# A three-stage attention and feed-forward kernel: another order of loads, operand splitting and cluster similarities ahead of the first attention step

## The chip, the cores and the metric

One core of one Trainium2 chip. The metric is the device time of one execution in microseconds (us); the time before is the median of 3 runs. In the traces PE is the matrix engine, PEld its weight loads, DVE the vector engine, ACT the scalar engine, POOL the GpSimd engine and SP the engine that only issues transfers. A q behind a name (SPq, POOLq) is that engine's instruction queue.

## What is computed

Three stages in one launch, in float32. The cut below shows the first, which the change is in; the other two are a low-rank token mixing with a ReLU feed-forward, and a feed-forward gated by a convolution.

```python
# q, k, v: (2, 8, 768, 64); centroids: (8, 16, 64)
q_assign = np.argmax(np.einsum('bhsd,hcd->bhsc', q_n, c_n), axis=-1)   # rows normalised
k_assign = np.argmax(np.einsum('bhsd,hcd->bhsc', k_n, c_n), axis=-1)
mask = q_assign[:, :, :, None] == k_assign[:, :, None, :]
scores = np.where(mask, scale * (q @ k.transpose(0, 1, 3, 2)), -1e9)
attn = softmax(scores)
x = (attn @ v), heads side by side           # (2, 768, 512)
u = x + (x.T @ U @ V).T;  y = u + relu(u @ w_ch1) @ w_ch2
h = relu(y @ w_in);       out = (h * sigmoid(conv3(h))) @ w_out
```

## The kernel before, in words

There are 2 batches of 8 heads; two neighbouring heads form a **pair**, so there are 8 pairs (p 0 to 3 of batch 0, then of batch 1). A head has 768 queries in 6 tiles of 128, so attention has 96 **steps**, 12 for a pair; step n is written out by `step(n)` (L545). The schedule is written by hand: each engine runs its instructions in the order of the program text and stops at the first one whose inputs are not there.

Products of float32 numbers are made from a rounded part (the type fp32r, written high) and the exact rest (low). For a head the scores' operands lie in two tiles. `ab` (128 rows) holds, for q and k, one high part and one low rest; `cd` (80 rows) holds the high parts and 16 more rows, the one-hot of the cluster that a token belongs to. A score tile is two matmuls on `ab` (L250) and two on `cd` (L252), summed in one bank pair `sc`; one for each half of the 768 keys.

A pair's operands come about so:

- `load_raw` (L87): three SP transfers bring the pair's q rows (`rq`, 384 KB) and k rows (`rk`, two of 192 KB on 64 partitions each).
- `load_ops` (L96): three POOL transfers, of 384 KB at the source each, bring one head's rows as fp32r into `ab` (twice) and `cd`. `split_ops` (L114) subtracts to get the low rests in `ab`.
- `sims` (L182): 24 small matmuls of `rq` and `rk` with the centroids (`cbq`, `cbk`) give the similarities. `sims_onehot` (L193) turns them into one-hots in five DVE operations, `onehot_t` (L212) transposes these on PE, and `onehot_rows` (L219) puts them into `cd`. For the first head of all (`first=True`) ACT writes both rows directly; otherwise ACT makes `os` and SP transfers move it.
- `load_v` (L105): one SP transfer (`rv`) and two POOL transfers (`vt`) for the values.

Ahead of the steps stands a prologue. SP loads the centroids and pair 0's rows; POOL makes `identf`, then issues the six `load_ops` transfers of heads 0 and 1 and two of `vt`. `warm(count)` (L134) issues that many matmuls whose result nothing reads, on zeroed data; there are 13 and 4 of them around the transpose of the centroids (L160) and 16 behind the similarities. DVE normalises the centroids, copies them into `cbq` and `cbk` (L163 to L166), writes constants (L169 to L177), makes head 0's low rests (L433 calls `split_ops` with DVE) and the one-hots. POOL makes head 1's low rests and those of `vt` (L436).

In step n the order on PE is: scores of n+2 (`s_mm`), value product of an earlier group (`pv_mm`), at s = 2 of a pair the similarities of the next pair (L563), and the transposes of n (`t_mm`, L280). DVE runs the low rests of n-1 (L293) and the score maximum of n+2 (`s_max`, L259); ACT the copies of n-1 (L289) and the exponential of n+1 (L271). `prep(n)` (L512) then issues what the next pair needs: s = 0 loads rows and the first head's operands, s = 2 to 5 one-hot parts, splits, `load_v` and the second head's operands, s = 7 the one-hot rows. `pump` moves the float64 weights of the later stages through SP, ACT, DVE and POOL, one piece at a time.

Of the kernel before, what the change touches and what calls it, by code (L numbers as in the profile page):

```python
# [15 lines left out]
F32 = mybir.dt.float32  # L16
# [8 lines left out]
P = 128  # L25
# Score offset that removes a key of another cluster. It exceeds every score by so
# much that a query whose cluster holds no key sees equal scores everywhere.
# [4 lines left out]
def tile_kernel(ctx: ExitStack, tc: tile.TileContext, qk, vv, cen, u_w, v_w, w1, w2, win, wout, conv, out):  # L32
# [20 lines left out]
    # ---- right side: u^T of the first batch, x rows, first weights, staging  # L53
# [9 lines left out]
    # ---- attention pools; the operands of the scores on top, to be freed first  # L63
# [18 lines left out]
    # ---------------------------------------------------------------- loads  # L82
# [12 lines left out]

    def load_ops(b, p, j):  # L96
        h = 2 * p + j
        ab = a_ab.tile([P, 2, S], F32R, tag="ab", name="ab")
        cd = a_ab.tile([80, 2, S], F32R, tag="cd", name="cd")
        nc.gpsimd.dma_start(out=ab[0:D], in_=qk[b, h])  # L100
        nc.gpsimd.dma_start(out=ab[D:2 * D], in_=qk[b, h])
        nc.gpsimd.dma_start(out=cd[0:D], in_=qk[b, h])
        ops[b, h] = (ab, cd)
# [17 lines left out]
    # ------------------------------------------------------------- constants  # L121
    cent = acon.tile([P, 2, D], F32, name="cent")
    nc.sync.dma_start(out=cent[:, 0], in_=cen)
    load_raw(0, 0)
    identf = const.tile([P, P], F32, name="identf")
    make_identity(nc, identf)
    load_ops(0, 0, 0)

    # TensorE runs at half its clock until it has been busy for a few microseconds
# [14 lines left out]
    # centroids, normalised, transposed into block-diagonal stationaries  # L144
# [7 lines left out]
    nc.scalar.activation(early, cn[:, 1:2], AF.Exp)  # brings Exp's table in before the scores  # L152
# [15 lines left out]
    identb = const.tile([P, P], BF16, name="identb")  # L168
    nc.vector.tensor_copy(identb, identf)  # L169
    iota = acon.tile([P, NT * 4, NC], BF16, name="iota")  # L170
    for c in range(NC):
        nc.vector.memset(iota[:, :, c:c + 1], float(NC - c))
    ohs = acon.tile([2 * 2 * NC, 2], F32, name="ohs")
    nc.vector.memset(ohs[0:2 * NC, 0:1], 1.0)
    nc.vector.memset(ohs[0:2 * NC, 1:2], 0.0)
    nc.vector.memset(ohs[2 * NC:4 * NC, 0:1], BIG)
    nc.vector.memset(ohs[2 * NC:4 * NC, 1:2], -BIG)  # L177

    # ------------------------------------------- cluster assignment of a pair
# [13 lines left out]
    def sims_onehot(b, p, part):  # L193
        """One-hot of the first largest similarity, in five parts."""
        sh = [P, NT * 4, NC]
        v = ohst[b, p]
        if part == 0:
            v["mx"] = a_oh.tile([P, NT * 4, 1], F32, tag="mx", name="mx")
            nc.vector.tensor_reduce(out=v["mx"], in_=v["pm"], axis=AX.X, op=ALU.max)
        elif part == 1:  # L200
            v["eq"] = a_oh.tile(sh, BF16, tag="eq", name="eq")
            nc.vector.tensor_tensor(out=v["eq"], in0=v["pm"], in1=v["mx"].to_broadcast(sh), op=ALU.is_ge)
        elif part == 2:
            nc.vector.tensor_tensor(out=v["eq"], in0=v["eq"], in1=iota, op=ALU.mult)
        elif part == 3:
            v["m2"] = a_oh.tile([P, NT * 4, 1], BF16, tag="m2", name="m2")
            nc.vector.tensor_reduce(out=v["m2"], in_=v["eq"], axis=AX.X, op=ALU.max)
        else:
            v["oh"] = a_oh.tile(sh, BF16, tag="oh", name="oh")
            nc.vector.tensor_tensor(out=v["oh"], in0=v["eq"], in1=v["m2"].to_broadcast(sh), op=ALU.is_equal)  # L210
# [8 lines left out]
    def onehot_rows(b, p, first=False):  # L219
        pt = ohst.pop((b, p))["pt"]  # L220
        if first:
            cd = ops[b, 2 * p][1]
            nc.scalar.activation(cd[D:D + NC, 0], pt[0:NC], AF.Copy)
            nc.scalar.activation(cd[D:D + NC, 1], pt[2 * NC:3 * NC], AF.Copy, scale=BIG, bias=-BIG)  # L224
        os_ = a_oh.tile([4 * NC, S], F32R, tag="os", name="os")
        nc.scalar.activation(os_, pt, AF.Identity, scale=ohs[:, 0:1], bias=ohs[:, 1:2])
        for j in range(1 if first else 0, 2):
            cd = ops[b, 2 * p + j][1]
            for i in range(2):
                r0 = (2 * i + j) * NC  # L230
                nc.sync.dma_start(out=cd[D:D + NC, i].bitcast(F32), in_=os_[r0:r0 + NC].bitcast(F32))

    # ----------------------------------------------------- attention, by steps
# [10 lines left out]
    def s_mm(n):  # L244
        b, h, t = head_of(n)
        ab, cd = ops[b, h]
        ps = ps_s.tile([P, 2, 512], F32, tag="s", name="sc")
        c0 = t * P
        for f in range(2):
            nc.tensor.matmul(ps[:, f, 0:HS], ab[:, 0, c0:c0 + P], ab[:, 1, f * HS:(f + 1) * HS], start=True, stop=False)  # L250
        for f in range(2):
            nc.tensor.matmul(ps[:, f, 0:HS], cd[0:80, 0, c0:c0 + P], cd[0:80, 1, f * HS:(f + 1) * HS], start=False, stop=True)  # L252
        st["s", n] = ps
# [85 lines left out]
    # ------------------------------------------------------------- weights  # L339
    # The parameters come as float64 words (low, high). The high word read as a  # L340
    # float32 and scaled by 2^-112 has the exponent rebased; shifted left by three
    # and joined with the sign and the low word's top bits it is the float32.
# [39 lines left out]
    # stages by ticks after a block's start: thinly spread, or one block every two ticks  # L382
# [3 lines left out]
    def pump(plan):  # L386
        """Moves every parameter block in flight on by a tick and starts the next one."""
# [37 lines left out]
    # ------------------------------------------------- the attention schedule  # L425
    sims(0, 0)
    load_ops(0, 0, 1)
    split_ops(0, 0, 0, nc.vector)
    warm(16)
    for part in range(5):  # L430
        sims_onehot(0, 0, part)
    onehot_t(0, 0)
    onehot_rows(0, 0, first=True)  # L433
    rv0 = load_v(0, 0)
# [3 lines left out]
    # parameters of the later stages  # L438
# [20 lines left out]
    # ---- token mixing, u = x + V^T (U^T x), and u^T split: in units that share a bank  # L459
# [52 lines left out]
    def prep(n):  # L512
        """Work for the next pair of heads, spread over this pair's twelve steps."""
        pair, s = divmod(n, 2 * NT)
        nxt = pair + 1
        if nxt < B * NP:
            b, p = divmod(nxt, NP)
            for part, at in enumerate((2, 2, 3, 4, 5)):
                if s == at:
                    sims_onehot(b, p, part)  # L520
            if s == 0:
                load_raw(b, p)
# [22 lines left out]
    def step(n):  # L545
# [17 lines left out]
        if s == 2 and n < NQ and pair + 1 < B * NP:  # L563
# [32 lines left out]
    # ---- u + relu(u W1) W2, in quarters of the hidden features  # L596
# [43 lines left out]
    def ffn():  # L640
        """Yields after each hidden tile and each accumulation."""
# [46 lines left out]
    # ---- h = relu(x Win), gated by its convolution, times Wout  # L688
# [126 lines left out]
```

## Time and profile before

| | us |
|---|---|
| median of 3 runs (698.17 to 699.41) | 698.79 |
| the profiled execution, first to last instruction (its span) | 696.7 |
| what lies around the span, by the median | 2.1 |
| PE busy in the span | 675.5 (97%) |
| DVE busy | 455.8 (65%) |
| ACT busy | 370.4 (53%) |
| POOL busy | 297.0 (43%) |

The profile gives the span of the profiled execution and no other time for it. PE's row says that it is busy nearly everywhere; where it is not can be read only stage by stage. Starts in the trace are counted from the span's beginning.

### The profile page before, as it was taken

How to read it: one execution, taken by the hardware profiler on the slowest of the kernel's cores; microseconds unless marked ns; L12 is line 12 of the kernel's file. 1: busy time of each engine (PE TensorE's matmuls, PEld its weight loads, DVE VectorE, ACT ScalarE, POOL GpSimd, SP SyncE). 2: the span in 40 equal slices, each digit the busy share in tenths (PEclk: the TensorE clock that was granted, in tenths of full speed). 3: DMA queues.
4: the chain of work that ended last, by engine and by line, in shares of the span. 5: the costliest groups of instructions: out<-in, count | busy, mean ns of one | idle time of the engine just before them, and what ended most of it. 6: DMA issues, size and time to landing. Idle time of an engine off the chain costs nothing.

```text
span 696.7 us, 11035 instructions
## 1 busy us (share of the span) xinstructions
PE 675.5 (97%) x4078; PEld 643.7 (92%) x4078; DVE 455.8 (65%) x859; ACT 370.4 (53%) x741; POOL 297.0 (43%) x370
## 2 busy tenths in 40 slices
PE   5699999999999999999999999999999999999997
PEld 4499999989898999899999999999999999998886
DVE  3577888888888888857933777775268435643400
ACT  1468888788888798615311333342134347653511
POOL 3448667767666551533630333332046334332300
PEclk8889999999999999999999999999999999999999
DMA  9577587666766620302200333331013000000111
GB/s 200 127 145 166 102 184 146 146 158 121 174 115 152 124 77 1 122 24 98 93 31 29 123 122 132 139 122 61 0 62 121 1 1 0 1 31 15 37 55 45
DMA packets 30342, 62.80 MB, mean 90 GB/s; under 512 B 15664, under 2 KB 15792, under 8 KB 30288
## 3 DMA queue, kind: packets, MB, share of 16 engines
q1 hardware_dynamic: 13904, 40.08, 18.0%
q0 software_dynamic: 16384, 22.02, 18.0%
q8 instruction: 32, 0.52, 0.3%
q14 instruction: 22, 0.18, 0.1%
HBM read 57.47 MB, written 3.15 MB: 87 GB/s over the span
## 4 chain that ended last, share of the span: by engine, by line
PE 86%; DVE 7%; DMA 2%; ACT 2%; issue 1%; SPq 1%; DVEq 0%; ACTq 0%
PE g L706 10%; PE pv L304 7%; PE tr L280 7%; PE h L608 6%; PE h L609 6%; PE h L610 6%; PE a L624 6%; PE a L625 6%; PE a L623 6%; PE sc L250 4%; PE sc L252 4%; PE sim L187 4%; PE po L741 3%; PE po L740 3%; PE po L739 3%; DMA rk<-in_qk_dram 2%
## 5 line engine op out<-in xcount | busy, mean ns | idle before, releaser
L613 ACT ACTIVATE rh<-h 128x384 fp32r<-128x384 f32 x64 | 31.5, 492 | 161.0 <-PE h L610 161.0
L418 POOL TENSOR_TENSOR wl<-wx,wh 128x512 fp32r<-128x512 f32 x48 | 65.2, 1358 | 115.8 <-ACT wh L417 101.4
L293 DVE TENSOR_TENSOR pl<-tr,ph 128x384 fp32r<-128x384 f32 x192 | 97.6, 549 | 19.5 <-ACT ph L289 18.4
L289 ACT CAST ph<-tr 128x384 fp32r<-128x384 f32 x192 | 83.6, 487 | 25.6 <-PE tr L280 25.1
L259 DVE TENSOR_SCALAR_CACHE_REDUCE e<-sc 128x768 f32<-128x768 f32 x96 | 90.7, 946 | 4.4 <-PE sc L252 4.4
L271 ACT ACTIVATE e<-sc,nb 128x768 f32<-128x768 f32 x96 | 88.1, 918 | 3.4 <-DVE e L259 2.9
L280 PE MATMUL tr<-identf,e 128*128 128x128 f32 x576 | 84.4, 278 | 3.0 <-DVE pl L293 1.2
L614 DVE SCALAR_TENSOR_TENSOR rl<-h,rh 128x384 fp32r<-128x384 f32 x64 | 35.5, 555 | 78.9 <-ACT rh L613 78.9
L608 PE MATMUL h<-uh,wh 128*128 128x384 f32 x256 | 86.0, 336 | 0.5 <-DVE rl L614 0.5
L623 PE MATMUL a<-rh,wh 128*128 128x384 f32 x256 | 85.9, 336 | 0.0
L610 PE MATMUL h<-uh,wl 128*128 128x384 f32 x256 | 85.6, 334 | 0.0
L625 PE MATMUL a<-rh,wl 128*128 128x384 f32 x256 | 85.6, 334 | 0.0
L624 PE MATMUL a<-rl,wh 128*128 128x384 f32 x256 | 85.6, 334 | 0.0
L609 PE MATMUL h<-ul,wh 128*128 128x384 f32 x256 | 85.6, 334 | 0.0
L280 PEld LDWEIGHTS tr<-identf,e 128*128 128x128 f32 x576 | 67.3, 143 | 11.5 <-DVE pl L293 6.5
L367 DVE SCALAR_TENSOR_TENSOR wx<-wb,wx 128x512 int32<-128x512 int32 (+3 forms) x52 | 59.8, 1151 | 10.3 <-ACT wb L358 8.7
L304 PE MATMUL pv<-ph,vt 128*128 128x384 f32 x192 | 65.4, 341 | 0.2 <-ACT asb L313 0.2
L304 PE MATMUL pv<-pl,vt 128*128 128x384 f32 x192 | 65.0, 338 | 0.0
L250 PE MATMUL sc<-ab 128*128 128x384 f32 x192 | 57.8, 382 | 1.7 <-ACT e L271 1.4
L722 POOL TENSOR_TENSOR h<-h,cv 128x768 f32<-128x768 f32 x16 | 29.6, 1850 | 65.0 <-ACT cv L721 65.0
L252 PE MATMUL sc<-cd 80*128 80x384 f32 x192 | 49.8, 341 | 1.2 <-ACT cd L224 1.2
L608 PEld LDWEIGHTS h<-uh,wh 128*128 128x128 f32 x256 | 48.0, 188 | 0.7 <-DVE rl L614 0.7
(124 smaller groups left out, 1496.7 us busy)
## 6 DMA issues: line engine op xcount, KB each, us to landing
raw<-in_w_dram SPq DMA_DIRECT2D x32, 512.0 KB, 3.4
ab<-in_qk_dram POOLq DMA_DIRECT2D x32, 384.0 KB, 5.5
cd<-in_qk_dram POOLq DMA_DIRECT2D x16, 384.0 KB, 6.9
raw<-in_win_dram SPq DMA_DIRECT2D x8, 512.0 KB, 3.2
raw<-in_wout_dram SPq DMA_DIRECT2D x8, 512.0 KB, 3.5
rq<-in_qk_dram SPq DMA_DIRECT2D x8, 384.0 KB, 4.0
rk<-in_qk_dram SPq DMA_DIRECT2D x16, 192.0 KB, 5.3
vt<-in_vv_dram POOLq DMA_DIRECT2D x16, 192.0 KB, 3.7
```

The source lines that it names most:

```text
L250: nc.tensor.matmul(ps[:, f, 0:HS], ab[:, 0, c0:c0 + P], ab[:, 1, f * HS:(f + 1) * HS], start=True, stop=False)
L259: nc.vector.tensor_scalar(out=e, in0=ps[:, :, 0:HS], scalar1=-SCALE, scalar2=3e38, op0=ALU.mult, op1=ALU.min, accum_out=nb,)
L271: nc.scalar.activation(e, ps[:, :, 0:HS], AF.Exp, scale=SCALE, bias=nb, accum_out=st["sum", n // 3][:, n % 3:n % 3 + 1])
L280: nc.tensor.transpose(pt[:, k, :], e[:, i, k * P:(k + 1) * P], identf)
L293: nc.vector.tensor_sub(lo, st.pop(("t", n, i)), hi)
L304: nc.tensor.matmul(acc, vt[:, h % 2, k, :], m[:, k].rearrange("p a b -> p (a b)"), start=(k == 0 and i == 0), stop=(k == NT - 1 and i == 1),)
L608: nc.tensor.matmul(ph, wh[:, k, ws], uh[b][:, k, ts], start=(k == 0), stop=False)
L609: nc.tensor.matmul(ph, wh[:, k, ws], ul[b][:, k, ts], start=False, stop=False)
L610: nc.tensor.matmul(ph, wl[:, k, ws], uh[b][:, k, ts], start=False, stop=(k == ND - 1))
L623: nc.tensor.matmul(accs[d], wh[:, i, ds_], rh, start=(f == 0), stop=False)
L624: nc.tensor.matmul(accs[d], wh[:, i, ds_], rl, start=False, stop=False)
L625: nc.tensor.matmul(accs[d], wl[:, i, ds_], rh, start=False, stop=(f == NH - 1))
```

## The change

It rewrites the prologue and takes pair 1's row loads and similarities out of the steps of pair 0. Only comments fall away besides.

```diff
+    def take_ops(b, p, j):
+        ab = a_ab.tile([P, 2, S], F32R, tag="ab", name="ab")
+        cd = a_ab.tile([80, 2, S], F32R, tag="cd", name="cd")
+        ops[b, 2 * p + j] = (ab, cd)
+        return ab, cd
...
     nc.sync.dma_start(out=cent[:, 0], in_=cen)
     load_raw(0, 0)
+    load_raw(0, 1)
     make_identity(nc, identf)
-    load_ops(0, 0, 0)
+    identb = const.tile([P, P], BF16, name="identb")
+    nc.gpsimd.tensor_copy(identb, identf)
+    iota = acon.tile([P, NT * 4, NC], BF16, name="iota")
+    for c in range(NC):
+        nc.gpsimd.memset(iota[:, :, c:c + 1], float(NC - c))
+    ohs = acon.tile([2 * 2 * NC, 2], F32, name="ohs")
+    nc.gpsimd.memset(ohs[0:2 * NC, 0:1], 1.0)
+    nc.gpsimd.memset(ohs[0:2 * NC, 1:2], 0.0)
+    nc.gpsimd.memset(ohs[2 * NC:4 * NC, 0:1], BIG)
+    nc.gpsimd.memset(ohs[2 * NC:4 * NC, 1:2], -BIG)
...
-    nc.vector.tensor_copy(identb, identf)
...
-        nc.vector.memset(iota[:, :, c:c + 1], float(NC - c))
-    nc.vector.memset(ohs[0:2 * NC, 0:1], 1.0)
...
+    rq0, rk0 = raw[0, 0]
+    ab0, cd0 = take_ops(0, 0, 0)
+    nc.scalar.copy(cd0[0:D, 0], rq0[0:D])
+    nc.scalar.copy(cd0[0:D, 1], rk0[D:2 * D])
+    nc.scalar.copy(ab0[D:2 * D, 0], rq0[0:D])
+    nc.scalar.copy(ab0[0:D, 1], rk0[D:2 * D])
+    nc.gpsimd.tensor_copy(ab0[D:2 * D, 1], rk0[D:2 * D])
+    nc.gpsimd.tensor_sub(ab0[D:2 * D, 1], rk0[D:2 * D], ab0[D:2 * D, 1])
+    nc.gpsimd.tensor_sub(ab0[0:D, 0], rq0[0:D], cd0[0:D, 0])
...
     if first:
         cd = ops[b, 2 * p][1]
-        nc.scalar.activation(cd[D:D + NC, 0], pt[0:NC], AF.Copy)
         nc.scalar.activation(cd[D:D + NC, 1], pt[2 * NC:3 * NC], AF.Copy, scale=BIG, bias=-BIG)
+        nc.vector.tensor_copy(cd[D:D + NC, 0], pt[0:NC])
...
     sims(0, 0)
+    sims(0, 1)
     load_ops(0, 0, 1)
-    split_ops(0, 0, 0, nc.vector)
-    warm(16)
+    rv0 = load_v(0, 0)
     for part in range(5):
         sims_onehot(0, 0, part)
+    s_mm_ab(0)
+    s_mm_ab(1)
+    warm(4)
     onehot_t(0, 0)
     onehot_rows(0, 0, first=True)
-    rv0 = load_v(0, 0)
+    warm(4)
+    for part in range(2):
+        sims_onehot(0, 1, part)
     split_ops(0, 0, 1, nc.gpsimd)
```

The lines under `if first:` are in `onehot_rows`. `s_mm_ab(n)` is the first half of `s_mm(n)`, the two matmuls on `ab`; `s_mm` issues it itself unless it has been issued. In `prep` the row loads, and parts 0 and 1 of the one-hots, are left out for pair 1; in `step` its similarities are. The POOL transfers of head 0's operands fall away; those of head 1 and of `vt` stay, and now stand on POOL behind the copy and the two subtractions of head 0. The matmuls of `warm` are 13, 4, 4 and 4 where they were 13, 4 and 16.

## Rows read from the trace of the kernel before

**Rows 1.** The page's first line.

```profile
span 696.7 us, 11035 instructions
```

**Rows 2.** Stretches for PE: length, busy (instructions), granted clock, DMA share, GB/s.

```profile
5.80:9.00 3.20, 0.41 (x3) 1.00 1.25 236
10.50:11.00 0.50, 0.00 (x0) 0.72 1.13 197
12.80:17.50 4.70, 4.70 (x23) 0.50 2.22 203
17.50:20.90 3.40, 3.40 (x12) 0.50 0.34 22
20.90:21.90 1.00, 1.00 (x7) 0.97 0.00 0
34.60:38.00 3.40, 3.40 (x19) 0.50 1.14 204
```

**Rows 3.** Chain that ended last, first 22.4 us: start, length, what.

```profile
2.24 10.42 DMA rk<-in_qk_dram
...
17.67 4.28 PE idle L136 x16
21.95 0.47 PE oht L216 x6
```

**Rows 4.** PE's timeline: start, length, what; releaser in brackets.

```profile
5.09 0.81 PE L136 MATMUL idle<-busy 128*128 128x384 bf16 x4
...
41.69 0.60 PE L250 MATMUL sc<-ab 128*128 128x384 f32 x2
...
66.58 0.30 PE L187 MATMUL sim<-cbq,rq 128*128 128x32 f32 x2
...
68.96 0.39 PE L187 MATMUL sim<-cbk,rk 128*128 128x32 f32 x2
```

**Rows 5.** DVE's timeline, same columns.

```profile
6.01 0.23 DVE L166 COPY cbk<-pc 64x64 f32<-64x64 f32 x1
...
17.71 0.56 DVE L199 TENSOR_REDUCE mx<-sim 128x24 f32<-128x384 f32 x1 [4.36 <-PE sim L187]
...
20.29 1.46 DVE L210 TENSOR_TENSOR oh<-eq,m 128x384 bf16<-128x384 bf16 x1
24.76 0.96 DVE L259 TENSOR_SCALAR_CACHE_REDUCE e<-sc 128x768 f32<-128x768 f32 x1 [3.01 <-PE sc L252]
...
29.62 0.95 DVE L259 TENSOR_SCALAR_CACHE_REDUCE e<-sc 128x768 f32<-128x768 f32 x1
...
31.43 0.94 DVE L259 TENSOR_SCALAR_CACHE_REDUCE e<-sc 128x768 f32<-128x768 f32 x1
...
41.04 0.96 DVE L259 TENSOR_SCALAR_CACHE_REDUCE e<-sc 128x768 f32<-128x768 f32 x1 [0.21 <-PE sc L252]
```

**Rows 6.** DMA issues, KB and us to landing; the third: all 16 issues of L101.

```profile
cent<-in_cen_dram SPq DMA_DIRECT2D x1, 32.0 KB, 1.7
...
raw<-in_w_dram SPq DMA_DIRECT2D x32, 512.0 KB, 3.4
...
DMA to landing us min/median/max: 5.1/5.9/13.8
```

**Rows 7.** Instruction groups by form: busy us, mean ns, idle before.

```profile
L728 ACT CAST gh<-h 128x768 fp32r<-128x768 f32 x16 | 13.4, 838 | 3.4 <-POOL h L722 3.4
L224 ACT ACTIVATE cd<-oht 16x768 fp32r<-16x768 bf16 x1 | 0.8, 800 | 0.0
L445 POOL COPY u<-wx 128x192 f32<-128x192 f32 x3 | 0.9, 346 | 0.0
L119 POOL TENSOR_TENSOR ab<-rq,ab 64x768 fp32r<-64x768 f32 x15 | 27.3, 1818 | 48.1 <-DMA ab<-in_qk_dram 36.9 <-issue 11.2
L110 POOL DMA_DIRECT2D vt<-in_vv_dram x16 | 13.9, 880 | 4.8 <-PE pv L304 4.8
masks.py:197 POOL MEMSET identf<- 128x128 f32 x1 | 0.2, 206 | 0.3 <-POOLq L801 0.3
```

More of the change, by code (lines that the diff above doesn't have):

```diff
@@ L94, in load_raw @@
         raw[b, p] = (rq, rk)
+    def take_ops(b, p, j):
[3 more added lines that the diff above has]
+        return ab, cd
     def load_ops(b, p, j):
         h = 2 * p + j
-        ab = a_ab.tile([P, 2, S], F32R, tag="ab", name="ab")
-        cd = a_ab.tile([80, 2, S], F32R, tag="cd", name="cd")
+        ab, cd = take_ops(b, p, j)
         nc.gpsimd.dma_start(out=ab[0:D], in_=qk[b, h])
@@ L102, in load_ops @@
         nc.gpsimd.dma_start(out=cd[0:D], in_=qk[b, h])
-        ops[b, h] = (ab, cd)
     def load_v(b, p):
@@ L166, in tile_kernel @@
     nc.vector.tensor_copy(cbk[D:2 * D, :, 0:NC], pcv[D:2 * D, :, 0])
-    identb = const.tile([P, P], BF16, name="identb")
-    nc.vector.tensor_copy(identb, identf)
-    iota = acon.tile([P, NT * 4, NC], BF16, name="iota")
-    for c in range(NC):
-        nc.vector.memset(iota[:, :, c:c + 1], float(NC - c))
-    ohs = acon.tile([2 * 2 * NC, 2], F32, name="ohs")
-    nc.vector.memset(ohs[0:2 * NC, 0:1], 1.0)
-    nc.vector.memset(ohs[0:2 * NC, 1:2], 0.0)
-    nc.vector.memset(ohs[2 * NC:4 * NC, 0:1], BIG)
-    nc.vector.memset(ohs[2 * NC:4 * NC, 1:2], -BIG)
+    rq0, rk0 = raw[0, 0]
[7 more added lines that the diff above has]
+    nc.gpsimd.tensor_sub(ab0[0:D, 0], rq0[0:D], cd0[0:D, 0])
     ohst = {}
@@ L242, in head_of, with s_mm_ab @@
         return b, h, t
-    def s_mm(n):
+    def s_mm_ab(n):
         b, h, t = head_of(n)
-        ab, cd = ops[b, h]
+        ab, _ = ops[b, h]
         ps = ps_s.tile([P, 2, 512], F32, tag="s", name="sc")
@@ L250, in s_mm @@
             nc.tensor.matmul(ps[:, f, 0:HS], ab[:, 0, c0:c0 + P], ab[:, 1, f * HS:(f + 1) * HS], start=True, stop=False)
+        st["s", n] = ps
+    def s_mm(n):
+        b, h, t = head_of(n)
+        if ("s", n) not in st:
+            s_mm_ab(n)
+        ps = st["s", n]
+        _, cd = ops[b, h]
+        c0 = t * P
         for f in range(2):
             nc.tensor.matmul(ps[:, f, 0:HS], cd[0:80, 0, c0:c0 + P], cd[0:80, 1, f * HS:(f + 1) * HS], start=False, stop=True)
-        st["s", n] = ps
     def s_max(n):
@@ L518, in prep @@
             for part, at in enumerate((2, 2, 3, 4, 5)):
-                if s == at:
+                if s == at and (nxt > 1 or part > 1):
                     sims_onehot(b, p, part)
             if s == 0:
-                load_raw(b, p)
+                if nxt > 1:
+                    load_raw(b, p)
                 load_ops(b, p, 0)
@@ L562, in step @@
             got = mix[0]()
-        if s == 2 and n < NQ and pair + 1 < B * NP:
+        if s == 2 and n < NQ and 1 < pair + 1 < B * NP:
             sims(*divmod(pair + 1, NP))
```

## The prediction, made before the changed kernel was run

> **What bounds the kernel now.** I read the page first: PE is busy 97% of a span of 696.7 us [rows 1]; the sum below is made against that span, and the median of the runs lies 2.1 above it. A kernel so full can be shortened only where PE is idle, slow or doing work that nobody reads, so next I cut the first 60 us into stretches for PE, with the granted clock, and followed the chain that ended last through them. Two holes lie there. The first reaches from the centroids to the first scores. The chain hangs for 10.42 us on a transfer of k rows issued at 2.24, then runs pair 0's similarities, 16 warm matmuls and the one-hot transposes [rows 3]. PE has nothing from 5.9, where warm's last four end [rows 4], to 12.8. While it idles the clock falls to half inside 10.5 to 11.0 (a mean of 0.72: 0.22 us at full, so at 10.7), the similarities run at half, and 3.4 us of warm pass before it is back [rows 2]. The first score maximum starts at 24.76 [rows 5]. The second hole is pair 1's similarities inside step 2: four maxima follow closely (the last two 1.81 apart), then the next comes at 41.04 instead of 33.24 [rows 5]. From there on PE is full, so I take what the prologue and step 2 save as saved at the end.
>
> **The change part by part.**
>
> *Loads.* On SP the three transfers of pair 1, some 1.7 us of issue by the spacing of pair 0's, and `rv` stand behind pair 0's; nothing else waits there until `os`. What goes is the company: eight POOL transfers, six of operands and two of `vt`, that pair 0's rows now share the engines with. In the shared stretch the rate is 236 GB/s [rows 2]. A transfer of 512 KB lands 1.7 us after the time that one of 32 KB takes [rows 6], some 289 GB/s, as the other end. Take 250: pair 0's 786 KB from 1.17 plus the 1.7 of a small transfer are in at 6.0 (5.6 to 6.3), pair 1's at 9.1 (8.3 to 9.6). `cbk` is ready at 6.24 [rows 5], so the similarities start at 6.3, not 12.8.
>
> By the Trainium skill, "SBUF — State Buffer", section "Door 1: The DMA port swizzle", rows on 64 partitions move at 196 GB/s where 128 reach 328; no run here isolates that. An estimate by that page puts pair 1's k rows some 0.7 us later, at 9.8, and the forecast near 685.
>
> *Similarities.* At full clock 24 matmuls take 2.7 us (66.58 to the end of the last at 69.35, which overlaps the next work) [rows 4]; at half twice that. Pair 0's end at 9.0; pair 1's start at 9.1. Does the clock hold? Similarities alone did not raise it: 4.7 us of them stayed at 0.50, as did 34.6 to 38.0, while warm raised it [rows 2]. In the change nothing but similarities runs from 6.3 on. I take the fall at 10.7 as before: 1.6 us of pair 1's are done, the remaining 1.1 take 2.2, and they end at 12.9. A fall at 9.1 would cost another 1.6; none would end them at 11.8.
>
> *Head 0's operands on chip.* ACT copies 64x768 four times; its 128x768 cast takes 0.84 [rows 7], so 3.4 in all, done before 9.5. POOL copies once: from 0.35 (the 128x192 copy) to 1.82 (a 64x768 subtraction); I take 0.9, a single-input copy scaled by less than its length. Two subtractions add 3.6: done at 10.6 (10.0 to 11.5). Hidden behind the similarities; if they end at 11.8 the slack is 1.2. The DVE subtractions and POOL transfers that it replaces give back nothing by themselves: the chain does not pass through them, it hangs on `rk` [rows 3]. The constants on POOL, 16 memsets of at most 0.2 [rows 7], a copy of at most 0.35 and four short ones, sum to 4.0 behind `identf` and are done by 5.5, while POOL would wait for `rk` anyway; without that cover they would cost up to 4. On DVE, where they leave, they ran in the wait before 17.71 [rows 5].
>
> *From there to the first maximum.* The four early `ab` matmuls have warm's width: 4/16 of 4.28 [rows 3], 1.1, most of it at half clock. Warm's next four take 1.1 as well: PE is at 15.1. The one-hots need 4.04 from the similarities' end (17.71 to 21.75) [rows 5], so 13.1, hidden. Transposes at half cost 0.9, at 16.0. Then the two `cd` rows are written side by side, on ACT 0.8 [rows 7] and on DVE between 0.8 and the 0.96 of a 768-wide read of a bank [rows 5]; I take 0.85, where ACT alone took 1.6. Warm's last four run beside it. But DVE now has parts 0 and 1 of pair 1 ahead of the first maximum: 2 x 0.6 (0.56 [rows 5] and a gap). First maximum at 16.9 + 1.2 = 18.1, against 24.76: **6.7 saved**. The clock is back about then, 3.4 us after dense matmuls start at 12.9.
>
> *Step 2 without similarities.* 41.04 - 33.24 = **7.8 saved** [rows 5]; what is late next is DVE, whose maxima, rests and remaining one-hot parts fill its steps; head 1's `os` transfers and the first weight piece follow on SP, with ten us and four before anyone wants them. The price is bounded by 0.6 less (parts of DVE work that idled there) and by nothing more.
>
> *Sum.* 6.7 + 7.8 = 14.5: a span of 682.2, a median of **684.3**.
>
> **Rivals.**
>
> *The clock holds* through the similarities. For: they run back to back, and at 66.58 they ran at full clock [rows 4], though between dense matmuls. Against: the 8 us in which they did not raise it [rows 2]. Then 11.8 + 0.55 + 0.55 = 12.9, transposes wait for the one-hots at 13.1 and end at 13.6, the maximum starts at 13.6 + 0.85 + 1.2 = 15.6: 9.2 + 7.8 = 17.0 saved, **681.8**. The Trainium skill, "TensorE: Matmul & The Clock Gate", section "HAM oscillation", ties the fall to idle gaps of the engine; by it this case happens. The trace agrees for the fall at 10.7 and shows no stretch of similarities alone that began at full clock. Chance 0.32.
>
> *Pair 0's rows land no sooner*, because the long `rk` transfer was slow for another reason than its company, so that the change does not do what it says. Then the similarities start at 12.8 again, POOL's chain ends at 17.4 and everything is 6.5 later: 8.0 saved, **690.8**. Against it: six such transfers stood in the shared stretch together. Chance 0.08.
>
> *Head 1's operands become late.* Their POOL issues, 3 at 0.55, moved behind POOL's chain: 10.6 to 12.3, `vt` to 14.1 (2 x 0.88) [rows 7]. With the median landing of 5.9 the split starts at 17.1 and, two at 1.82 and `vt`'s third, all is done at 22.6; scores of step 6, now at 41.69 [rows 4], would want it at 27.2, values 0.8 later. With the longest landing, 13.8 [rows 6], `vt` is done at 30.5, 2.5 late: **686.8**. Against it: the long landing had eight transfers beside it. Chance 0.06.
>
> *Slower.* Half clock stays on in the steps. A step has eight matmuls as wide as warm's and six transposes, by warm's 0.27 and the 0.9 above at least 3.1 at half and 1.5 less at full, where the maxima stand 1.81 apart [rows 5]. Each such step so adds 1.5, and from the tenth on the 14.5 are spent. With all 12 steps of pair 0 at half, 18.4 are added: **702.7**. For it: similarities no longer follow a long warm, and the first steps have gaps. Against it: dense matmuls raised the clock within 3.4 us [rows 2]. Chance 0.03.
>
> **How the numbers follow.** The forecast has 0.50 (the last 0.01 is for no change). Its own terms reach from 682.7 (the fall comes late, fast transfers) to 686.5 (a fall at 9.1 and slow transfers); the held clock, with the one-hots 0.3 sooner, gives 681.5. Either end is moved out by the 1.2 between the lowest and the highest run of before: from 680.3 to 688.0, which holds these two and late operands at 686.8, 0.88 less their tails; it leaves out late rows and the slower case. About 0.2% (1.4 us) is what a measurement of this kernel can tell from none. All but the last two cases are faster: 0.96; within 0.2% 0.01; slower 0.03.
>
> **What would show it.** Right: PE's similarities of both pairs start near 6.3 and 9.1; the granted clock reads 0.5 before 12; the first maximum starts near 18, no similarity stands in step 2, and maxima 4 and 5 stand under 2.5 us apart. If the clock reads 1.00 up to there, the second number holds. Wrong: PE's first wait ends on `rk` after 10; scores of step 6 waiting for `ab`, or values for `vt`; maxima over 3 us apart through several steps at 0.5.

## The result: 688.0 us, with the profile of the changed kernel

The changed kernel takes 687.99 us (median of four executions, 687.68 to 689.51) beside 698.93 for the kernel before in the same session: a ratio of 0.985, interval 0.983 to 0.987. That is faster, but 3.7 us above the forecast of 684.3. The median stands at the very top of the range (688.0), and the ratio (0.9851) applied to the 698.79 that the forecast started from gives 688.4, just above it. Two more sets of four further down give 690.0 and 690.1, each 7.7 below the kernel before in its session, where this one is 10.9 below; over all twelve executions (687.68 to 692.71) the median is 689.5. The profile is of the fastest of the twelve: its span of 685.9 is 10.8 shorter than that of [rows 1], against a forecast 14.5.

The page of the changed kernel, its first line and the first of its engines:

```profile
span 685.9 us, 11019 instructions
...
PE 674.6 (98%) x4070; PEld 642.8 (94%) x4070; DVE 451.7 (66%) x837; ACT 372.6 (54%) x744; POOL 301.9 (44%) x391
```

PE is as busy as before (674.6 us against 675.5), so of the 10.8 that the span lost, 9.9 went out of its holes. The chain that ended last, first 20 us (start, length, what):

```profile
4.02 5.60 DMA rk<-in_qk_dram
9.75 4.77 PE sim L201 x22
14.52 1.44 PE sc L264 x4
15.96 1.31 PE idle L150 x4
18.92 0.95 DVE cd L238
```

Where pair 0's `rk` stood in [rows 3] for 10.42 us, pair 1's now stands for 5.60, and ends 3.0 sooner. Behind it come 4.77 us of similarities, so at half clock. PE's timeline (start, length, what; releaser in brackets):

```profile
6.61 0.30 PE L201 MATMUL sim<-cbq,rq 128*128 128x32 f32 x2
...
9.21 0.39 PE L201 MATMUL sim<-cbq,rq 128*128 128x32 f32 x2
9.75 0.50 PE L201 MATMUL sim<-cbk,rk 128*128 128x32 f32 x2 [0.16 <-DMA rk<-in_qk_dram]
...
14.34 1.63 PE L264 MATMUL sc<-ab 128*128 128x384 f32 x4
15.77 1.50 PE L150 MATMUL idle<-busy 128*128 128x384 bf16 x4
17.20 0.85 PE L230 MATMUL oht<-identb,oh 128*64 128x128 bf16 x6
...
19.92 1.65 PE L275 MATMUL sc<-cd 80*128 80x384 f32 x4 [0.48 <-DVE cd L238]
```

PE in stretches (length, busy, granted clock, DMA share, GB/s):

```profile
8.00:9.00 1.00, 1.00 (x12) 1.00 1.09 230
9.00:10.00 1.00, 0.84 (x8) 0.94 0.80 252
10.00:11.00 1.00, 1.00 (x7) 0.50 0.00 0
...
16.00:18.00 2.00, 2.00 (x11) 0.50 2.64 159
...
26.00:27.00 1.00, 1.00 (x5) 0.53 1.14 283
27.00:28.00 1.00, 1.00 (x9) 1.00 1.11 246
```

A mean of 0.94 in the second is 0.88 us at full clock: the fall is at 9.9, in the middle of the similarities, with PE's one gap of 0.16 just before it. The clock is back at 26.9. ACT's timeline and DVE's between:

```profile
18.09 0.80 ACT L237 ACTIVATE cd<-oht 16x768 fp32r<-16x768 bf16 x1 [9.76 <-PE oht L230]
19.97 0.99 ACT L240 ACTIVATE os<-oht,ohs 64x768 fp32r<-64x768 bf16 x1 [1.08 <-DVE cd L238]
```

```profile
18.92 0.95 DVE L238 CAST cd<-oht 16x768 fp32r<-16x768 bf16 x1 [6.71 <-ACT cd L237]
19.90 0.56 DVE L213 TENSOR_REDUCE mx<-sim 128x24 f32<-128x384 f32 x1
20.49 0.56 DVE L216 TENSOR_TENSOR eq<-sim,mx 128x384 bf16<-128x384 f32 x1
20.97 0.96 DVE L281 TENSOR_SCALAR_CACHE_REDUCE e<-sc 128x768 f32<-128x768 f32 x1
...
29.01 0.95 DVE L281 TENSOR_SCALAR_CACHE_REDUCE e<-sc 128x768 f32<-128x768 f32 x1
...
30.88 0.95 DVE L281 TENSOR_SCALAR_CACHE_REDUCE e<-sc 128x768 f32<-128x768 f32 x1
```

The two `cd` rows do not run side by side: DVE's is released by the end of ACT's, and `os` by the end of DVE's. The first maximum starts at 20.97, 3.8 before that of [rows 5]; the fifth and the sixth, 29.01 and 30.88, stand 1.87 apart where they stood 9.61 apart.

### The profile page after: what moved, and what is told of

Same layout as the page of the kernel before. It is cut to its first block, busy times and chain, and to the rows that moved or that the text cites. A ratio compares the mean times of both kernels' runs of the same rounds, so it can differ in the third digit from the quotient of the medians.

```text
span 685.9 us, 11019 instructions
## 1 busy us (share of the span) xinstructions
PE 674.6 (98%) x4070; PEld 642.8 (94%) x4070; DVE 451.7 (66%) x837; ACT 372.6 (54%) x744; POOL 301.9 (44%) x391
## 3 DMA queue, kind: packets, MB, share of 16 engines
q0 software_dynamic: 16144, 20.84, 17.1%
## 4 chain that ended last, share of the span: by engine, by line
PE 87%; DVE 8%; ACT 2%; issue 1%; DMA 1%; SPq 0%; DVEq 0%; ACTq 0%
PE g L734 10%; PE pv L326 7%; PE tr L302 7%; PE h L636 6%; PE h L638 6%; PE h L637 6%; PE a L653 6%; PE a L651 6%; PE a L652 6%; PE sc L264 4%; PE sc L275 4%; PE po L768 3%; PE po L769 3%; PE po L767 3%; PE sim L201 3%; DVE pl L315 2%
## 5 line engine op out<-in xcount | busy, mean ns | idle before, releaser
L302 PEld LDWEIGHTS tr<-identf,e 128*128 128x128 f32 x576 | 67.0, 143 | 11.5 <-DVE pl L315 6.5
L389 DVE SCALAR_TENSOR_TENSOR wx<-wb,wx 128x512 int32<-128x512 int32 (+3 forms) x52 | 59.5, 1145 | 10.3 <-ACT wb L380 8.8
```

Source lines behind the costliest of these rows:

```text
L302: nc.tensor.transpose(pt[:, k, :], e[:, i, k * P:(k + 1) * P], identf)
```

## The experiments

Every run is read by one scale. The **lead** of a run at the n-th score maximum is the start of that maximum in [rows 5]'s profile less its start in the run's. Behind the 95th the lead is the final one: for the changed kernel it is 10.8, and so is the difference of the spans. In the table stand the leads in us, the median, its executions, and the ratio to the kernel before in the same session with its interval. A lead is that of one execution, the profiled one. In the changed kernel, fill, rows_on_act, after_again, before_rows_feed and fill_feed_u that was the fastest of its set, in sims_in_step2, feed_only, clock_held and fill_feed_u_again the slowest, so a lead shows where time goes, and the median what an edit is worth. "Feed" is short for head 2's operand transfers issued in the prologue, "u_w" for the first weight piece's transfer there.

| run | 1st | 5th | 7th | 14th | 95th | us (executions) | ratio |
|---|---|---|---|---|---|---|---|
| changed kernel | 3.8 | 2.4 | 10.5 | 10.4 | 10.8 | 688.0 (687.7–689.5) | 0.985 (0.983–0.987) |
| fill | 6.5 | 4.4 | 12.5 | 10.5 | 10.5 | 689.8 (687.9–691.1) | 0.990 (0.988–0.992) |
| sims_in_step2 | 7.0 | 5.5 | 10.3 | 9.5 | 9.2 | 688.3 (687.5–689.3) | 0.987 (0.985–0.989) |
| rows_on_act | 4.8 | 2.9 | 10.9 | 10.6 | 11.2 | 689.8 (687.2–691.4) | 0.989 (0.986–0.992) |
| pool_early | −1.5 | −3.5 | 4.6 | 4.6 | 5.5 | 693.1 (692.5–694.3) | 0.995 (0.993–0.996) |
| after_again | 4.2 | 2.3 | 10.3 | 10.1 | 10.8 | 690.0 (687.7–692.7) | 0.989 (0.986–0.993) |
| feed_only | 2.6 | 0.8 | 8.7 | 7.1 | 7.4 | 688.7 (687.1–691.1) | 0.988 (0.985–0.990) |
| fill_feed | 6.3 | 5.2 | 11.4 | 9.8 | 9.6 | 687.8 (686.4–689.2) | 0.986 (0.983–0.988) |
| clock_held | −0.1 | −0.1 | 8.0 | 8.0 | 8.0 | 689.9 (689.6–690.5) | 0.989 (0.988–0.991) |
| fill_feed_u | 6.5 | 5.6 | 13.6 | 13.6 | 14.0 | 686.0 (684.4–691.4) | 0.985 (0.982–0.988) |
| feed_u_act | 4.7 | 2.6 | 10.8 | 10.8 | 10.2 | 688.0 (683.2–690.3) | 0.986 (0.983–0.989) |
| before_rows | 0.8 | 0.8 | 6.6 | 1.0 | 1.1 | 698.2 (696.2–699.3) | 1.000 (0.999–1.002) |
| before_rows_feed | 1.5 | 0.3 | 6.2 | 6.2 | 6.6 | 693.6 (691.9–697.3) | 0.995 (0.993–0.997) |
| after_third | 2.4 | 1.6 | 9.0 | 9.0 | 8.0 | 690.1 (689.5–691.3) | 0.989 (0.988–0.990) |
| fill_feed_u_again | 5.7 | 3.8 | 11.8 | 11.8 | 11.9 | 685.8 (684.7–686.6) | 0.983 (0.981–0.984) |
| fill_feed_u_act | 6.9 | 5.0 | 13.0 | 13.0 | 12.9 | 685.7 (685.4–685.9) | 0.983 (0.981–0.984) |

The time came outside what was expected in nine runs: above it in fill, sims_in_step2, rows_on_act, pool_early, feed_only, fill_feed, clock_held and before_rows, and after_again gained 7.7 where 10 to 11.5 were expected. In sims_in_step2 and before_rows the rival's time came out, but not by its mechanism: step 2 did shrink in both.

**Does something denser keep the clock?** A warm matmul after each tile of both prologue similarities:

```diff
-    def sims(b, p):
+    def sims(b, p, fill=0):
...
+            warm(fill)
...
-    sims(0, 0)
-    sims(0, 1)
+    sims(0, 0, fill=1)
+    sims(0, 1, fill=1)
```

> The changed kernel with one warm matmul after each of the six tiles of both prologue similarities (12 in all). Theory, the clock: it fell at 9.9 because similarities alone did not hold it, and came back only at 26.9. With warm work mixed in it stays at 1.00; a tile takes 0.45 + 0.16, both similarities 7.3, so they end at 13.9 instead of 14.5 although there is more to do; early scores and warm 1.4, transposes 0.5, the two cd rows 1.8, two one-hot parts 1.2: first maximum at 18.8 instead of 21.0, and the first five maxima 6.7 apart in all instead of 8.0. Time 684.5. Rival, the wait for pair 1's k rows at 9.6 lets it fall: the clock falls all the same, the 12 cost up to 3.8 at half: 690 to 692.

PE in stretches, run fill:

```profile
10.00:11.00 1.00, 1.00 (x12) 1.00 0.17 65
14.00:16.00 2.00, 2.00 (x16) 1.00 1.23 242
16.00:18.00 2.00, 0.89 (x5) 1.00 2.20 179
18.00:20.00 2.00, 0.20 (x2) 0.98 2.36 147
20.00:22.00 2.00, 1.69 (x6) 0.50 0.46 123
```

The clock stays at 1.00 until 20, and falls there after a stretch with PE mostly idle. The first maximum gains 2.7. Yet the final lead is no larger than that of the changed kernel: 2.1 go in the first steps, at half clock from 20 on (the changed kernel loses 1.4 there), and 2.0 between the seventh maximum and the fourteenth. POOL's timeline and DVE's of fill show where the largest part of the 2.0 goes, 1.3 at the eighth maximum:

```profile
29.78 2.00 POOL L123 TENSOR_TENSOR ab<-rq,ab 64x768 fp32r<-64x768 f32 x1 [5.42 <-DMA ab<-in_qk_dram]
31.86 1.82 POOL L123 TENSOR_TENSOR ab<-rk,ab 64x768 fp32r<-64x768 f32 x1
```

```profile
32.26 1.53 DVE L386 TENSOR_SCALAR wx<-raw 128x192 int32<-128x192 int32 x1
```

Head 2's split waits 5.42 for its transfers and now lies on DVE's weight word: 1.53 us, ended just after POOL's subtraction at 33.68, where the changed kernel's took 0.37 and that of fill_feed_u 0.25, both with no POOL subtraction beside them. PE waits 1.05 for DVE right behind it. By the Trainium skill, "SBUF — State Buffer", section "Who interferes with whom", DVE and GpSimd share a pair of ports that one of them holds for a whole instruction; the durations agree.

In the five profiles with fill whose similarities began at full clock (fill, fill_feed, both of fill_feed_u, fill_feed_u_act) it stayed up through all of them, also behind a wait of 0.99 for rows. In eight of the nine without fill that run both pairs' similarities in the prologue it fell inside them, at 8.5 to 11.4; in the ninth, pool_early, it fell at 10.6 in a wait. In the profile above PE had waited 0.16 until then, so idle time is not what told them apart. Whether it is the width of the inserted matmul or its type (bf16 against float32) was not tried.

**The similarities back in step 2** (rows still early, parts 0 and 1 too):

```diff
-    sims(0, 1)
...
-    for part in range(2):
-        sims_onehot(0, 1, part)
...
-                if s == at and (nxt > 1 or part > 1):
+                if s == at:
...
-        if s == 2 and n < NQ and 1 < pair + 1 < B * NP:
+        if s == 2 and n < NQ and pair + 1 < B * NP:
```

> The changed kernel with pair 1's similarities and one-hot parts 0 and 1 back in step 2; its rows still load early. Theory, the clock: what cost 7.8 in step 2 was the wait for rows and the clock that fell in it, not the similarities. In the prologue pair 0's end at 9.3, PE waits for POOL until 10.2, early scores and warm end at 11.6, transposes 12.7, cd rows 14.5, first maximum 15.0 (6.0 sooner); step 2 pays 2.7 for the similarities at full clock: 3.3 to 5 less in all, 683 to 684.7. Rival, standing back to back in the prologue is what pays: step 2 is stretched by 6 to 8 again and the time is 688 to 690.

DVE's timeline of sims_in_step2:

```profile
17.75 0.96 DVE L281 TENSOR_SCALAR_CACHE_REDUCE e<-sc 128x768 f32<-128x768 f32 x1 [1.10 <-PE sc L275]
...
25.91 0.95 DVE L281 TENSOR_SCALAR_CACHE_REDUCE e<-sc 128x768 f32<-128x768 f32 x1
...
30.08 0.95 DVE L281 TENSOR_SCALAR_CACHE_REDUCE e<-sc 128x768 f32<-128x768 f32 x1
```

The first maximum comes at 17.75, 2.8 later than expected: the clock fell here too, at 10.4, while PE waited for the early scores. Step 2 with similarities at full clock costs 2.3 (fifth to sixth maximum 4.17 apart against 1.87). So of the 7.7 that step 2 saves, 5.4 are rows that are there and a clock that is up, and 2.3 the similarities' other place; those are paid for in the prologue. Their place is worth 0.2 of lead at the seventh maximum and 1.6 at the end, and no time that is told apart.

**Both rows on ACT.**

```diff
-            nc.vector.tensor_copy(cd[D:D + NC, 0], pt[0:NC])
+            nc.scalar.activation(cd[D:D + NC, 0], pt[0:NC], AF.Copy)
```

> The changed kernel with both cd rows of head 0 written by ACT again. Theory: the DVE copy does not run beside ACT's but waits for it, because both read the transposes' bank, so DVE gains nothing and its two one-hot parts are held up behind it. ACT needs 2 x 0.8, DVE is free for the parts before: first maximum at 20.4 instead of 21.0, 687.4. Rival, the copy on DVE is a help and waits for something else: first maximum at 21.6, 688.6.

Lead 1.0 more at the first maximum and 0.2 to 0.5 more later; the time is not told apart from the changed kernel's. Of the 1.0, 0.5 lies ahead of the rows, where its clock fell 0.9 later, and 0.4 behind them, where its clock was up again when the `cd` scores ran.

**Company for the rows.** Head 1's operand transfers issued on POOL ahead of head 0's split:

```diff
     nc.gpsimd.memset(ohs[2 * NC:4 * NC, 1:2], -BIG)
+    load_ops(0, 0, 1)
...
-    load_ops(0, 0, 1)
     rv0 = load_v(0, 0)
```

> The changed kernel with head 1's three POOL transfers issued right behind the constants, ahead of head 0's copy and subtractions. Theory, company: the long landing of k rows in the kernel before came from POOL transfers in the same stretch. Three of them from 3.6 on bring it back in part: pair 0's k rows land 0 to 1.5 later than 5.6, pair 1's at 11 to 13 instead of 9.6, first maximum 1 to 3 later, 689 to 691. Rival, the landing is set by SP's own order: nothing moves there, 688.0.

PE's timeline of pool_early:

```profile
14.92 0.61 PE L202 MATMUL sim<-cbk,rk 128*128 128x32 f32 x2 [5.05 <-DMA rk<-in_qk_dram]
```

Three POOL transfers at the side put pair 1's k rows from 9.75 to 14.92. So the prediction's reason for the first hole, the company of POOL transfers, holds, and the rows are in later than the 11 to 13 that was expected.

**The changed kernel again, the feed, and both with fill.** The feed is

```diff
     rv0 = load_v(0, 0)
+    load_ops(0, 1, 0)
...
                 if nxt > 1:
                     load_raw(b, p)
-                load_ops(b, p, 0)
+                    load_ops(b, p, 0)
```

> The changed kernel once more, unaltered, as the measure for the other runs of this group: the maxima stand 10 to 11 us before those of the kernel before from the seventh on, 10 to 11.5 less in time. Theory and rival agree.

> The changed kernel with head 2's transfers issued in the prologue and nothing else. Theory, POOL: with the late first maximum head 2's rows were in at 26.5, early enough, so the lead at the fourteenth maximum moves by less than 0.5 from 10.4; 687.5 to 688.2. Rival, POOL holds back the changed kernel too: 1 to 2 less.

> The run with warm matmuls among the similarities, and the transfers of head 2's operands issued in the prologue behind those of head 1, not in step 0. Theory, POOL: there the maxima stood 12.5 us early at the seventh and 10.5 at the fourteenth, because POOL's split of head 2 waited for its transfer to 29.8, then stood in DVE's way and came late to all that follows it. With the rows there in time the split follows at 23 to 25 and the 12.5 are kept within 0.5: 685 to 686 where the unaltered one takes 688. Rival, the steps themselves fill DVE and ACT and give back any lead: 10.5 at the fourteenth as before, 688.

The clock falls at 10.8 in after_again, before 9.0 in feed_only. The four executions of after_again, one and the same program, differ by 5 us. In fill_feed the weight piece is next: its transfer lands 8.5 us after its issue at 19.68, ACT's L381 waits 1.79 for it, and the clock falls a second time. The feed alone brings no time that can be told.

**Everything at once**: fill, feed, both rows on ACT, and 9 warm matmuls behind the rows and 8 behind the first scores.

```diff
-    warm(4)
+    warm(9)
...
             s_mm(n + 2)
+        if n == -1:
+            warm(8)
```

> Warm among the similarities, head 2's transfers early, both cd rows on ACT, 9 warm matmuls where PE waits for the cd rows and 8 where it waits for the first exponential. Theory, clock and POOL together are what the forecast's 17.0 lacked: the clock stays at 1.00 through the first steps, first maximum at 17.4, the sixth 8.5 behind it at 25.9, lead 15 there and 14 at the fourteenth: 684. Rival, warm only costs PE time and the steps are bound by DVE: lead 11 at the fourteenth, 688.

PE waited 1.62 for pair 0's `rk` after its first matmul, and the clock fell before 7.9. PE in stretches, run clock_held:

```profile
7.00:8.00 1.00, 0.14 (x1) 0.92 1.11 227
8.00:10.00 2.00, 2.00 (x11) 0.50 1.02 194
...
16.00:18.00 2.00, 2.00 (x12) 0.50 2.05 197
```

Here filled similarities that began at half clock, at 7.9, were still there when they ended at 19.6; the same instructions held the clock in fill. So in these two profiles the fill keeps a clock and does not bring one back. The three executions that were not profiled have a mean granted clock of 0.994 to 0.995, as fill's have, and are no faster (689.6 to 690.0, the profiled one 690.5 at 0.989). So the run does not show that a held clock gives time: the added warm matmuls may cost what it saves, and no profile shows where.

**Fill, feed, and the weight piece early**; then the same without fill and with both rows on ACT; and the kernel before with pair 1's rows alone.

```diff
     rv0 = load_v(0, 0)
+    u_job = {"src": [(0, u_w.rearrange("p t r -> p (t r)"))], "put": lambda x: put_u(x)}
+    job_dma(u_job)
+    u_job.update(at=-1, plan={k: f for k, f in THIN.items() if k})
+    fly.append(u_job)
+    load_ops(0, 1, 0)
...
-    jobs.append({"src": [(0, u_w.rearrange("p t r -> p (t r)"))], "put": put_u})
```

`job_dma` issues the transfer; the other two lines leave the rest of the piece's work to `pump`.

> Warm among the similarities, head 2's transfers early, and the first weight piece's transfer (u_w) issued in the prologue behind the values, not in step 0. Theory, transfers: a lead won in the prologue is lost between the sixth and the fourteenth maximum because transfers of pair 1 and u_w then come too late; with head 2's early the ACT wait on u_w (1.8 us) took the place of POOL's. With both early the lead at the sixth, 12 to 12.5, is 11.5 to 12 at the fourteenth: 686. Rival, DVE and ACT fill these steps and give the lead back whatever lands: 10.4 at the fourteenth, 688.

> The changed kernel without warm among the similarities, with head 2's transfers and u_w early and both cd rows on ACT. Theory, clock first: without fill the clock falls between 9 and 11, the first maximum stands at 20 to 21 and the lead at the fourteenth is 10.5 to 11: 687.5, no better than the changed kernel. Rival, transfers are all that matters: lead 12, 686.

For before_rows, in the kernel before:

```diff
     load_raw(0, 0)
+    load_raw(0, 1)
...
-                load_raw(b, p)
+                if nxt > 1:
+                    load_raw(b, p)
```

> The kernel before with one part of the change alone: pair 1's three row transfers issued in the prologue behind pair 0's. Theory: the 7.8 us of step 2 were mostly the wait for these rows and the clock that fell in it. The first maximum stays within 1 us of 24.8 (its rows are ahead on SP's queue but share the engines), step 2 pays 2.7 for the similarities at full clock and gives back 4 to 5: 694 to 695. Rival, the similarities themselves are the cost of step 2: 697 to 699.

In fill_feed_u the lead of 13.6 at the seventh maximum is still there at the fourteenth. Without the fill it is 10.8 and kept too. One execution of fill_feed_u took 691.4, and its mean granted clock is 0.990 where the other five have 0.994 to 0.998. One of feed_u_act took 683.2, the shortest of all, at 0.997 where the others have 0.988 to 0.990: it can have had no more than some 4 us at half clock (an estimate: 0.003 of 681, doubled), so similarities without fill do not lose the clock for long in every execution.

In before_rows the rows alone win 5.5 in step 2 and lose it again: 1.6 at the eighth maximum, 4.0 at the thirteenth and the fourteenth. POOL's timeline, DVE's and PE's of before_rows:

```profile
38.13 1.81 POOL L119 TENSOR_TENSOR ab<-rq,ab 64x768 fp32r<-64x768 f32 x1 [5.53 <-DMA ab<-in_qk_dram]
```

```profile
38.21 1.86 DVE L364 TENSOR_SCALAR wx<-raw 128x192 int32<-128x192 int32 x1
```

```profile
54.26 0.76 PE L253 MATMUL sc<-cd 80*128 80x384 f32 x2 [2.46 <-DMA cd<-os]
```

The first is fill's case again: head 2's split comes late and lies on a DVE weight word. The second is a one-hot row of pair 1 that landed late, with PE at half clock behind the wait.

**On one chip: the changed kernel, the best version, and what keeps the lead.** before_rows_feed is before_rows with the feed; fill_feed_u_act is fill_feed_u with both rows on ACT.

> The changed kernel once more, beside the two below on the same chip. Theory (the loss against the forecast is made ahead of the first maximum and in the steps at half clock, and differs with the moment at which the clock falls): 686.5 to 690.5, the median near 688.3; the lowest maximum of a score comes between 20 and 22.5 and the lead over the kernel before, 10 to 11 at the seventh maximum, stays as it is to the end. Rival (the loss is made later, in the steps of pair 1): the lead at the seventh maximum is over 12 and shrinks by 2 or more up to the fourteenth.

> Warm matmuls among the similarities, head 2's transfers and the u_w transfer in the prologue, once more. Theory (a held clock saves some 2.5 at the first maximum, and the early transfers let pair 0's steps keep it): 685 to 686.5, 1.5 to 3 below the changed kernel beside it, the lead at the seventh maximum 12.5 to 14 and the same at the fourteenth. Rival (the first timing was a lucky one, and executions scatter by more than the edit is worth): the intervals of the two overlap and the medians differ by under 1.

> The kernel before, with pair 1's rows and head 2's operand transfers in its prologue; the similarities stay in step 2, head 0 is still split from POOL transfers. Theory (step 2's hole is the late rows, and a lead is lost again only where the next transfers come late): the sixth maximum leads by 5 to 6.5 as with the rows alone, and with head 2's operands early 4 to 6 of it are still there at the fourteenth: 692.5 to 695. Rival (the lead was lost to something that the operands do not feed: the one-hot rows, the weight words): the lead at the fourteenth is 0 to 2 again and the time 697 to 698.5.

> As the run with warm matmuls among the similarities and both early transfers, and both one-hot rows of head 0 written by ACT, so that DVE's parts 0 and 1 of pair 1 are done beside them. Theory (two serial rows and then two parts stand on DVE ahead of the first maximum; on ACT the rows cost 1.6 and the parts run beside them): first maximum 0.5 to 1.1 earlier, 17.2 to 17.8, and 0.5 to 1 faster than that run. Rival (DVE's rows wait for ACT's only because the same bank is read, and two ACT rows take as long as one of each): the first maximum comes within 0.3 of 18.3 and the time within 0.5.

The best version, fill_feed_u, is 4.3 below the changed kernel beside it, where 1.5 to 3 were expected, and no execution of the one (684.7 to 686.6) reaches one of the other (689.5 to 691.3): it beats both kernels. In its first set of six one execution, the 691.4, did reach them. The mean granted clock of its four executions here is 0.995 to 0.997, of the changed kernel's 0.984 to 0.990. after_third confirms that the changed kernel keeps its lead from the seventh maximum to the fourteenth, at 9.0 where 10 to 11 were expected (1.0 goes later): its clock fell at 8.5, in the similarities again. What goes later goes at the thirtieth maximum. DVE's timeline of after_third:

```profile
93.36 2.18 DVE L389 SCALAR_TENSOR_TENSOR wx<-wb,wx 96x384 int32<-96x384 int32 x1
```

POOL subtracts beside it, from 93.30 to 95.13; in the first profile of the changed kernel the same instruction starts at 91.92, as POOL's subtraction ends (91.96), and takes 0.54. PE waits 1.38 for DVE behind it, and the lead is 1.6 smaller. feed_only (691.1) loses 1.6 so at its ninth maximum: a one-hot part of 2.19 at 38.03, in the prologue 0.56, beside a POOL subtraction from 37.98 to 39.80. So in these two profiles part of the scatter is which DVE instruction POOL's subtractions happen to meet.

With the feed, before_rows keeps all 6.2 of its lead in the profiled execution, its fastest. The median of its eight lies 4.2 below the kernel before, but three of them (696.6 to 697.3) have spans only 1 to 2 shorter than [rows 1], so they had little of it left at the end. The rows on ACT bring the first maximum to 17.85 (18.31 and 19.11 in the two runs without), but no time that can be told.

**Why DVE's row stood behind ACT's.** spare_row has both rows on ACT and DVE's copy of the transposes sent elsewhere; other_source has DVE's row from SBUF, and leaves out the one-hot row that belongs there:

```diff
-            nc.vector.tensor_copy(cd[D:D + NC, 0], pt[0:NC])
+            nc.vector.tensor_copy(ops[b, 1][1][D:D + NC, 0], pt[0:NC])
+            nc.scalar.activation(cd[D:D + NC, 0], pt[0:NC], AF.Copy)
```

```diff
-            nc.vector.tensor_copy(cd[D:D + NC, 0], pt[0:NC])
+            nc.vector.tensor_copy(cd[D:D + NC, 0], raw[0, 0][0][0:NC])
```

> The changed kernel with both rows of head 0 written by ACT, and DVE's copy of the same part of the transposes sent to the row of head 1 instead, which os's transfer overwrites later, so nothing reads it. Theory (what puts DVE's row behind ACT's is that both read the one tile of transposes): DVE's copy still starts only as ACT's row ends, 0.8 after the transposes are in, and ACT's second row starts only behind DVE's copy. Rival (it is that both write the tile cd): DVE's copy starts within 0.1 of ACT's first row.

> The changed kernel with DVE's row of head 0 copied from the query rows in SBUF instead of the transposes (left out: the query's one-hot row of head 0, so its scores are not the reference's). Theory (reading one tile is what orders the rows): DVE's copy waits for nothing and is done before the transposes, ACT's os follows ACT's row without a wait, and the first maximum starts 0.9 to 1.2 sooner behind the end of the transposes. Rival (writing one tile orders them): DVE's copy waits for the end of ACT's row as before, or ACT's row for DVE's copy.

ACT's timeline of spare_row, then DVE's of it, then ACT's of other_source:

```profile
19.30 0.80 ACT L237 ACTIVATE cd<-oht 16x768 fp32r<-16x768 bf16 x1 [10.87 <-PE oht L230]
21.11 0.80 ACT L239 ACTIVATE cd<-oht 16x768 fp32r<-16x768 bf16 x1 [1.02 <-DVE cd L238]
```

```profile
20.13 0.95 DVE L238 CAST cd<-oht 16x768 fp32r<-16x768 bf16 x1 [6.46 <-ACT cd L237]
```

```profile
18.70 0.80 ACT L237 ACTIVATE cd<-oht 16x768 fp32r<-16x768 bf16 x1 [9.95 <-PE oht L230]
19.53 0.99 ACT L240 ACTIVATE os<-oht,ohs 64x768 fp32r<-64x768 bf16 x1
```

It is the tile that is read: readers of the one tile of transposes on two engines go one after the other, whatever they write. Without the read, the first maximum (20.21) starts 1.51 after ACT's row does, in the changed kernel 2.88. DVE's timeline of other_source:

```profile
20.21 0.96 DVE L281 TENSOR_SCALAR_CACHE_REDUCE e<-sc 128x768 f32<-128x768 f32 x1 [3.63 <-PE sc L275]
```

Of the 1.37, 0.95 is DVE's row. The other 0.4 took two things: the two parts are done by then, and the `cd` scores ahead of the maximum run at full clock, so that it starts 0.66 after they do. At half clock it starts 1.05 after them, in the changed kernel (19.92 to 20.97) as in sims_in_step2 (16.70 to 17.75), which has no parts there. So in the changed kernel the parts were hidden beside these scores. One execution each: 692.1 for spare_row, 687.3 for other_source, beside 699.3 for the kernel before.

By the Trainium skill, "PSUM — Partial Sum Buffer", section "PSUM bank collisions raise a hardware error", two engines may not touch the same 32 partitions of a bank at once, though other partitions of it they may. These two rows lie in partitions 0 to 15 and 32 to 47, so by that page they need not wait for each other, and `os`, which reads 64, must; whether the first wait can be lifted was not tried.

## Why the prediction came out as it did

**Right.** *The first hole's cause.* Without the POOL transfers beside them pair 0's first k rows are in at 5.7 and PE, which starts at 6.6, never waits for the others (6.0 forecast); in after_again and after_third it does, until 7.2 and 7.3, still 5.5 sooner than before. Pair 1's are in at 9.6 (9.1 forecast). The 9.8 that the prediction estimates from the Trainium skill does not come out of the two rates that it takes from there: 384 KB of q rows and as much of k rows for each pair, from 2.87, would be in at 9.3, by an estimate. pool_early shows the same from the other side. *Head 0 on chip.* ACT's four copies end at 8.3, POOL's chain at 10.3 (10.6), the first copy 0.82 (0.9); the constants on POOL end at 3.5, in its wait for `rk`. *Head 1's operands.* The split starts at 16.7 and ends with `vt` at 22.2 (17.1 and 22.6); nobody waits for it. *Step 2.* 7.74 saved, 7.8 forecast. *The fall.* That similarities alone do not keep the clock was chosen against the rival that they do, and every profile of the changed kernel shows the fall inside them. *The premise.* Of the 10.2 won by the sixth maximum nothing is lost later: 10.8 at the end. That is one execution: in after_third 1.0 of 9.0 is lost, at a DVE instruction beside a POOL subtraction, a case to which the prediction gave no time.

**Wrong: the first maximum at 18.1, 6.7 saved.** It came at 20.97, and 2.9 are missing, in three terms. "The fall at 10.7 as before, ... they end at 12.9": the fall came at 9.9 and the similarities ended at 14.34, 1.4 later. 10.7 was taken over from an execution in which PE had been idle; here it is neither that nor a fixed time (8.5 to 10.8 in three profiles). Early scores, warm and transposes "at 16.0": 3.7 for 3.1, 0.6, for the clock was at half throughout and the 1.1 for four matmuls was an average over warm whose last microsecond ran at full clock. "The two `cd` rows are written side by side ... 0.85": 1.8, so 1.0. That term is a wrong mechanism, not a size: spare_row and other_source show the order. Only the two parts behind them were 0.1 cheaper, and beside them the `cd` scores at half clock, which the sum does not have, took as long.

**Wrong: "the clock is back about then".** It was back at 26.9, not 18.1. That dense matmuls raise it within 3.4 us was read from one stretch of one execution. From first to fifth maximum 8.04 pass where 6.67 did: 1.4 more. This is the mechanism of the slower rival at a smaller size: 0.7 in each of two steps (second to fourth maximum), where that rival had 1.5 in each of twelve. The sum had nothing for it. So 14.5 − 2.9 − 1.4 is 10.2, with step 2 as forecast, and 0.6 come back later: 10.8.

**The rivals.** The held clock was priced at 681.8. fill held it and did not get there: its similarities are longer by 0.08 a tile (0.53 against 0.45), PE waits 0.4 for the rows, and the two serial rows stand behind them, so its first maximum is at 18.27, not 15.6; its clock falls at 20 and the first steps run at half; and without the early transfers more is lost at a weight word. The rule of the Trainium skill, "TensorE: Matmul & The Clock Gate", section "HAM oscillation", on which that rival leaned ties the fall to idle gaps; the rows of this kernel, a fall at 9.9 with PE busy since 1.1 but for 0.16, do not agree.

**The range.** It allowed 1.2 for the scatter of executions. The changed kernel's twelve cover 5.0. The clock does not explain all of that: of four executions side by side in after_again, 687.7 and 692.0 have the same mean granted clock of 0.990. after_third and feed_only show one cause, a DVE instruction beside a POOL subtraction, at 1.6 a time; no profile was taken of the slowest executions.

## What to carry to other kernels

A lead won in an early step may be lost again where the next steps' transfers are not ready earlier too: before_rows won 6 and kept 1; with head 2's transfers early it kept 6, though not in every execution. Small matmuls in a row are to be costed at either clock: 48 of them in the prologue fell to half on the way in eight profiles of nine, 24 between dense matmuls (before_rows, step 2) did not, and a wide one after every four kept the clock up at 0.08 a tile where it was up to begin with. Where two engines read one PSUM tile, look whether they go one after the other, as here. And where DVE and POOL work side by side, one instruction of DVE can take four times as long, with PE behind it: 2.18 for 0.54.

## What was not expected of the hardware

That the clock falls under a busy PE: 9.9 in the changed kernel, with stretches of 1.00 busy on both sides. That dense matmuls bring it back at such different times: in after_third scores and warm from 16.07 had it back at 18.8; in the changed kernel scores, warm and transposes without a gap from 14.34 to 19.4 did not. PE in stretches, run after_third:

```profile
16.00:18.00 2.00, 2.00 (x8) 0.50 2.01 202
18.00:20.00 2.00, 2.00 (x14) 0.81 2.72 137
20.00:22.00 2.00, 0.89 (x5) 1.00 0.00 0
22.00:24.00 2.00, 0.24 (x2) 1.00 0.29 60
...
25.00:26.00 1.00, 1.00 (x9) 0.80 1.08 227
26.00:27.00 1.00, 1.00 (x6) 0.50 1.26 243
```

There it fell once more at 25.6, after PE had been busy for 1.1 of the four microseconds from 20 to 24. What decides the moment of a fall or a rise stays open.
